# A_log loaded as four rows and transposed by TensorE, with the weight transfers issued at other places

## The chip, the cores and the metric

The kernel runs on one NeuronCore of a Trainium2 chip. Times are device microseconds (us) of one execution. The runs of one version lie 1 to 3% apart from the fastest to the slowest, so each version was run four to six times, next to runs of the kernel before on the same chip in the same rounds. A run that is over 1.5% above the fastest run of its own version counts as slow and is left out of ratios. Every ratio below is the mean time of one kernel's fast runs over the mean of the other's fast runs of the same rounds, with a 95% interval, so it is not quite the ratio of the medians that stand beside it. "Slower" means more than 2%; where the interval spans 2%, the record calls the run unclear.

Engines are PE (TensorE matmul), PEld (its weight load), DVE (VectorE), ACT (ScalarE), POOL (GpSimd) and SP (SyncE, which here only issues DMAs).

## The reference, cut to what matters

An RWKV-like attention feeds a gated state-space layer:

```python
# attention; r, k, v, w: (4, 8, 768, 48) float32, u: (8, 48)
for t in range(S):
    cur = einsum('bhd,bhe->bhde', u[None] * kt, vt)
    y[:, :, t] = einsum('bhd,bhde->bhe', rt, state + cur)
    state = wt[:, :, :, None] * state + einsum('bhd,bhe->bhde', kt, vt)
# x = y as (4, 768, 384); w_in: (384, 1024), A_log: (512,), w_out: (512, 384)
proj = x @ w_in
val, gate = proj[..., :512], proj[..., 512:]
a = exp(A_log)
for t in range(S):
    h = a * h + val[:, t, :]
    ys[:, t, :] = h
return (silu(gate) * ys) @ w_out
```

A_log is 512 words, 2 KB, of the 23.80 MB that the SP queue moves. It is used for the first time by the first scan over h.

## The kernel before

The kernel is hand-scheduled. The 24 chunks of 128 steps (12 units of two) and the layer behind them are cut into small pieces of work, each with a letter, and one long string says in which order they are issued. Each piece goes to the queue of its engine, and each engine takes its queue in order. The letters that matter here: `w r k v` load a unit's w and a chunk's r, k, v (SP queue); `l` takes the logarithm of w (ACT); `c j` are cumulative sums of it (PE); `K` scales k by an exponential (POOL; `H` on DVE); `m u d V` make the bonus term (`m u V` on POOL, `d` on DVE); `A Y S T t` are attention matmuls and transposes (PE); `+` adds the bonus on DVE and `*` adds it through PE; `g n` are the projections with w_in (PE), `h` the scan, `o` the output projection; `W` issues a third of w_in (256 KB, on POOL's queue, cast to bf16 on the way), `X` half of w_out; `0` loads u and A_log, `a` takes exp of A_log; `#` is a filler matmul whose result nobody uses; it only keeps PE from standing idle. A number behind a letter, as in w3 or k5, counts its occurrences from 0: w3 is unit 3's w, k5 chunk 5's k.

```python
loads = ctx.enter_context(tc.tile_pool(name="loads", bufs=6))
...
w_in_sb = const.tile([128, NT, 2 * DI], BF16)
w_out_sb = const.tile([128, NG, DM], BF16)
a_log = const.tile([128, NG], F32)              # NG = 4: 16 bytes in each partition
a_sb = const.tile([128, NG], F32)
u_sb = const.tile([C, H, D], F32)
...
def load(n, un, ci):                            # k, r, v: runs of 48 words (192 B)
    if (n, un) not in raw:
        raw[n, un] = loads.tile([C, 2, H, D], F32, tag=n, name=n)
    t = dict(k=k, r=r, v=v)[n]
    nc.sync.dma_start(out=raw[n, un][:, ci], in_=bass.AP(..., ap=[[D, C], [S * D, H], [1, D]]))

def load_w(un):                                 # w: runs of 96 words (384 B)
    raw["w", un] = loads.tile([C, H, 2, D], F32, tag="w", name="w")
    nc.sync.dma_start(out=raw["w", un], in_=bass.AP(..., ap=[[2 * D, C], [S * D, H], [1, 2 * D]]))

def load_w_in(T):
    nc.gpsimd.dma_start(out=w_in_sb[:, T], in_=moe_w_in[T * 128 : (T + 1) * 128, :])

def load_small():
    nc.sync.dma_start(out=u_sb, in_=bass.AP(..., ap=[[0, C], [1, H * D]]))
    nc.sync.dma_start(out=a_log, in_=moe_A_log.rearrange("(g p) -> p g", p=128),
                      allow_slow_non_contiguous=True)
...
def f_a():
    nc.scalar.activation(a_sb, a_log, Exp)
```

## Time and profile before

| | before |
|---|---|
| median of 3 runs (range) | 139.37 us (138.71 to 139.43) |
| span of the profiled run | 137.9 us |
| PE busy | 128.1 us, 93% |
| TensorE clock granted | full throughout |
| packets of the SP queue | 91488, for 23.80 MB |

The prediction shows the lines that locate the bound: PE nearly without idle time after about 35 us, and before that a start set by loads. The time that the packets took as a share of 16 engines' span: every packet's time counts in full, so in a short window a share can pass 1.

```profile
q1 hardware_dynamic: 91488, 23.80, 76.6%
```

### The profile page before, as it was taken

The numbers are of one execution on the slowest core, as the hardware profiler recorded it, in microseconds if no ns is written. First come the engines' busy times: TensorE is split into PE (matmuls) and PEld (weight loads), VectorE is DVE, ScalarE is ACT, GpSimd is POOL, SyncE is SP. The second block draws the span as 40 slices with busy tenths as digits, with TensorE's granted clock in tenths as the row PEclk, the third lists the DMA queues.
The fourth block names the chain that finished last, engine by engine and source line by source line (L and its number), as shares of the span: only waits on it lengthen the run. The fifth ranks groups of instructions, "written<-read, shape, count | busy, mean of one in ns | idle before, by whom it ended". The sixth has DMA issues, their size and how long they took to land.

```text
span 137.9 us, 3768 instructions
## 1 busy us (share of the span) xinstructions
PE 128.1 (93%) x1433; PEld 78.7 (57%) x1441; DVE 114.4 (83%) x206; ACT 105.6 (77%) x208; POOL 111.2 (81%) x116
## 2 busy tenths in 40 slices
PE   5999997698899999999999999999999899999990
PEld 2345453465555554766456756766666476676850
DVE  1261698589898799989989999999999899999950
ACT  3350935874987799999998999999999998554451
POOL 7652559998696599999999999999899998405960
PEclk9999999999999999999999999999999999999999
DMA  4998979999898998999999899898958631011344
GB/s 88 287 203 161 217 140 234 192 227 251 172 243 164 193 246 166 243 216 213 193 211 223 168 209 302 164 207 222 305 165 179 152 125 57 0 57 62 114 165 177
DMA packets 92481, 25.21 MB, mean 183 GB/s; under 512 B 88368, under 2 KB 92080, under 8 KB 92464
## 3 DMA queue, kind: packets, MB, share of 16 engines
q1 hardware_dynamic: 91488, 23.80, 76.6%
q0 software_dynamic: 976, 1.18, 5.2%
q8 instruction: 11, 0.18, 0.5%
q14 instruction: 6, 0.05, 0.1%
HBM read 21.43 MB, written 4.72 MB: 190 GB/s over the span
## 4 chain that ended last, share of the span: by engine, by line
PE 59%; SPq 12%; DMA 9%; DVE 5%; POOL 5%; issue 3%; ACT 3%; ACTq 0%; DVEq 0%; POOLq 0%
PE bank L403 18%; PE bank L445 10%; SPq L190 10%; PE bank L310 5%; PE bank L233 4%; DMA w_in_sb<-in_moe_w_in_dram 4%; PE bank L323 4%; PE bank L99 3%; DMA r<-in_r_dram 3%; PE bank L345 3%; DVE bank L427 2%; PE bank L367 2%; DMA k<-in_k_dram 2%; PE bank L342 2%; PE bank L350 2%
## 5 line engine op out<-in xcount | busy, mean ns | idle before, releaser
L403 PE MATMUL bank<-xT,w_in_sb 128*128 128x384 bf16 (+2 forms) x216 | 38.4, 309 | 1.9 <-DMA w_in_sb<-in_moe_w_in_dram 1.0
L331 DVE TENSOR_TENSOR At<-bank,mask 128x512 bf16<-128x512 f32 x48 | 30.4, 682 | 0.5 <-PE bank L323 0.4
L99 PE MATMUL bank<-fill 128*128 128x512 bf16 x85 | 25.3, 410 | 1.9 <-DVE fill L91 1.5
L403 PEld LDWEIGHTS <-w_in_sb 128*128 128x128 bf16 x216 | 18.3, 98 | 11.3 <-DMA w_in_sb<-in_moe_w_in_dram 1.4
L283 POOL TENSOR_TENSOR rk<-rk,u_sb 128x768 f32<-128x768 f32 (+1 forms) x13 | 21.9, 1687 | 2.8 <-DMA u_sb<-in_u_dram 2.6
L278 POOL TENSOR_TENSOR rk<-r,k 128x768 f32<-128x768 f32 (+1 forms) x13 | 21.9, 1688 | 2.5 <-DMA k<-in_k_dram 2.5
L293 POOL TENSOR_TENSOR VD<-v,dv 128x768 f32<-128x768 f32 (+1 forms) x13 | 17.9, 1378 | 5.0 <-DVE dv L288 4.9
L272 POOL TENSOR_TENSOR Qb<-r,EQ 128x384 bf16<-128x384 f32 x19 | 19.0, 1002 | 2.7 <-ACT EQ L266 2.1
L172 ACT COPY qk<-bank 128x1024 bf16<-128x1024 bf16 x19 | 19.7, 1036 | 0.5 <-PE bank L310 0.3
L445 PE MATMUL bank<-w_out_sb,s 128*128 128x384 bf16 x96 | 18.9, 326 | 0.1
L414 ACT ACTIVATE s<-bank 128x384 bf16<-128x384 f32 (+2 forms) x36 | 15.7, 463 | 3.7 <-PE bank L403 3.5
L272 POOL TENSOR_TENSOR Kb<-k,EK 128x384 bf16<-128x384 f32 x17 | 16.9, 997 | 1.5 <-ACT EK L266 1.1
L172 ACT COPY o<-bank 128x384 f32<-128x384 f32 x23 | 11.4, 494 | 4.1 <-PE bank L445 2.8
L99 PEld LDWEIGHTS <-fill 128*128 128x128 bf16 x93 | 8.5, 103 | 10.3 <-issue 3.1
L225 ACT ACTIVATE lwb<-w 128x768 bf16<-128x768 f32 x12 | 10.3, 862 | 4.7 <-DMA w<-in_w_dram 4.6
L440 DVE TENSOR_TENSOR s<-s,bank 128x384 bf16<-128x384 bf16 x24 | 12.8, 547 | 1.2 <-ACT c L436 0.9
L440 POOL TENSOR_TENSOR s<-s,h 128x384 bf16<-128x384 bf16 (+2 forms) x12 | 7.6, 675 | 6.3 <-DVE h L427 6.3
L427 DVE TENSOR_TENSOR_SCAN bank<-a_sb,bank 128x384 f32<-128x384 f32 x12 | 11.3, 956 | 1.4 <-PE bank L403 0.7
L427 DVE TENSOR_TENSOR_SCAN bank<-a_sb,c,bank 128x384 f32<-128x384 f32 x12 | 12.0, 1013 | 0.6 <-PE bank L403 0.6
L392 DVE TENSOR_TENSOR SE<-bank,E 128x384 bf16<-128x384 f32 x20 | 11.0, 548 | 0.9 <-PE bank L384 0.9
L288 DVE TENSOR_REDUCE dv<-rk 128x16 f32<-128x768 f32 (+1 forms) x13 | 11.5, 883 | 0.2 <-POOL rk L283 0.2
L361 DVE TENSOR_TENSOR yb<-bank,VD 128x384 bf16<-128x384 f32 x20 | 11.0, 550 | 0.8 <-PE bank L350 0.8
(74 smaller groups left out, 240.5 us busy)
## 6 DMA issues: line engine op xcount, KB each, us to landing
r<-in_r_dram SPq DMA_DIRECT2D x24, 192.0 KB, 4.3
w<-in_w_dram SPq DMA_DIRECT2D x12, 384.0 KB, 4.6
k<-in_k_dram SPq DMA_DIRECT2D x24, 192.0 KB, 4.3
v<-in_v_dram SPq DMA_DIRECT2D x24, 192.0 KB, 4.1
out_dram<-o SPq DMA_DIRECT2D x24, 192.0 KB, 1.9
w_in_sb<-in_moe_w_in_dram POOLq DMA_DIRECT2D x3, 256.0 KB, 5.4
w_out_sb<-in_moe_w_out_dram POOLq DMA_DIRECT2D x2, 192.0 KB, 4.5
u_sb<-in_u_dram SPq DMA_DIRECT2D x1, 192.0 KB, 4.6
```

The lines of the kernel that those rows point to most:

```text
L99: nc.tensor.matmul(t, fill[:, :128], fill, start=True, stop=True, skip_group_check=True)
L172: (nc.scalar.copy if e == "ACT" else eng[e].tensor_copy)(dst, src)
L272: eng[e].tensor_tensor(dst[un % 3][:, ci, :, :D], raw[src, un][:, ci], tl[ex, i], op=MUL)
L278: eng[e].tensor_tensor(tl["rk", un][:, c0:c1], raw["r", un][:, c0:c1], raw["k", un][:, c0:c1], op=MUL)
L283: eng[e].tensor_tensor(t, t, u_sb[:, None].broadcast_to([C, c1 - c0, H, D]), op=MUL)
L293: nc.gpsimd.tensor_tensor(tl["VD", un][:, c0:c1], raw["v", un][:, c0:c1], tl["dv", un][:, c0:c1, :, None].broadcast_to([C, c1 - c0, H, D]) ...
L331: nc.vector.tensor_tensor(At[:, hh], tl["A", i][hh], mask[:, None, :].broadcast_to([C, NP, C]), op=MUL)
L403: nc.tensor.matmul(ps, w_in_sb[:, T, col : col + 128], xT[b][:, T, x[0] : x[1]], start=(T == 0), stop=(T == NT - 1))
L414: nc.scalar.activation(sg[b, g][:, x[0] : x[1]], tl["g", b, x, g], Silu)
L427: nc.vector.tensor_tensor_scan(dst, a_sb[:, g : g + 1].broadcast_to([128, n]), ps, 0.0 if x[0] == 0 else tl["c", b, g], op0=MUL, op1=ADD)
L440: (nc.gpsimd if b == B - 1 else nc.vector).tensor_tensor(s, s, tl["h", b, x, g], op=MUL)
L445: nc.tensor.matmul(ps[:, :DM], sg[b, g][:, tt * 128 : (tt + 1) * 128], w_out_sb[:, g, :], start=(g == 0), stop=(g == NG - 1))
```

## The change

The intent: 512 single words are a costly way to bring 2 KB, and they stand in the queue early, when loads set the pace. Four rows of 512 bytes, transposed by PE against an identity matrix, take their place. The weights go out earlier, so that the first gate projection no longer waits for them, and the whole order is arranged anew around that.

```diff
-    a_log = const.tile([128, NG], F32)
+    a_rows = const.tile([NG, 128], F32)
     a_sb = const.tile([128, NG], F32)
     u_sb = const.tile([C, H, D], F32)
...
-        nc.sync.dma_start(out=a_log, in_=moe_A_log.rearrange("(g p) -> p g", p=128),
-                          allow_slow_non_contiguous=True)
+
+    def load_a():
+        nc.sync.dma_start(out=a_rows, in_=moe_A_log.rearrange("(g p) -> g p", p=128))
+
+    def f_at():
+        tl["at"] = bank(512)[:, :NG]
+        nc.tensor.transpose(tl["at"], a_rows, ident32[:NG, :NG])
+
+    def f_a():
+        nc.scalar.activation(a_sb, tl["at"], Exp)
...
-    put("a", f_a)
+    for letter, fn in zip("LRa", (load_a, f_at, f_a)):
+        put(letter, fn)
... the order, first three of eleven lines
-    "rwwkrlv############cjrl2k##c1Q2Hk1Pm#####tv0Hmw##########tj2r31qkHuP2r3##########t1dAqvx"
-    "Vbk###AualP##YwxmSprus#######Avdcjx1k2K1HW2+Vld########TQ3#cPWt1etbHmq##SvqYstW+V1ApTAxy"
-    "ubkx#####SrYA+vjsT3xwy#Y2g2KdSkigPgrstV+iv#npbghwiniShKYClksm###AzrnzTCv*hjyuTvYx23lke2Q"
+    "wrvkwl############cjr2r1Q32Hkbmkl10############cPt1w1pKrHm#########tvjquAk32Wdr2PVxL####"
+    "###tvWAWbkP#Ylpmwx##S*#RAsrcuxj1vYau32TdkPvlVd1K#########cH2+###tePSqktKsp1##AV1txbTAqm#"
+    "Yx###Se*AKsrjxTuY32vy2w*d#######gkgiPSr#tVgpvinisgbwhniSKlhAkYmnsrzzCCv####TxjQyYv2+ulhk"
...
```

More of the change, by code (lines that the diff above doesn't have):

```diff
@@ L33 @@
 ORDER = (
-    "rwwkrlv############cjrl2k##c1Q2Hk1Pm#####tv0Hmw##########tj2r31qkHuP2r3##########t1dAqvx"
-    "Vbk###AualP##YwxmSprus#######Avdcjx1k2K1HW2+Vld########TQ3#cPWt1etbHmq##SvqYstW+V1ApTAxy"
-    "ubkx#####SrYA+vjsT3xwy#Y2g2KdSkigPgrstV+iv#npbghwiniShKYClksm###AzrnzTCv*hjyuTvYx23lke2Q"
-    "####jzC*rdn2QcrbhtVT1kYe31zgC2HwKip#gSQ+Avsgmxcirni1nhrtuSvhlkz1#####jQsqwzKdb###Ac3xk2Q"
-    "t1TY2rVp1ty+SvqAsmgrxlSAYvisKxk###TnK*kYbhtQwyTn+yuzqTthvgqAemrgzigdiXgixniVjlvhnKXcSzYh"
-    "Q1k2Cs2u3rz*#####YCH1Tckb+tQe1TdvSyA1xgvqnmgwisghnKrohCiSVbkozfztkiYsKCqA+vgxQnfriSlujhw"
-    "TozAemows2x32cfn>1KSdfrY1jbhQktl+VnrzqostvhfKY32T2+QoqzTeSQleAstrfQxgqAknmxigvtghrKgiAiv"
-    "zouqx>Yitkf+Auqdc>jk1xnoV>hn>1Y>2hKo2>3CTfzQjvyzACf+K>Y2xbt>Qov32+TSfmdnq>cstkyhS1Vn1rTz"
-    "CoqhuYyYsfgCzb>o+KvigdAQg+SxVfAio>ixtmfTY>ysnb+nhqQYohKTTfgzyu>Syzti+gqsAgdiAigxVSigxYin"
-    "o+sTnhyTfYy>nzghnigzgi+nhonhfzTo>yhzingohzifngh>gzginihfgnzii>nhnnzohznohfzh>ohzfhzo>Fzz"
-    "of>o>f>f>"
+    "wrvkwl############cjr2r1Q32Hkbmkl10############cPt1w1pKrHm#########tvjquAk32Wdr2PVxL####"
+    "###tvWAWbkP#Ylpmwx##S*#RAsrcuxj1vYau32TdkPvlVd1K#########cH2+###tePSqktKsp1##AV1txbTAqm#"
+    "Yx###Se*AKsrjxTuY32vy2w*d#######gkgiPSr#tVgpvinisgbwhniSKlhAkYmnsrzzCCv####TxjQyYv2+ulhk"
+    "###T2jyrzC3Q*d##n2rcbhtVk3T1Ye1pCwg2KzgiHmSvsAg+rix#ciQnk1ShunrthlvKz1####jwqzQd32###Ask"
+    "K2tbxcrTVY11tpryS+qmAsgvlxTSvAiYQskxK###nk*YyQhtwbTnu+ytzqgrhTgiXveqgzXAdmrgiinxivjlVSkh"
+    "nckhK#YC1z2Q2s1H#####Yu*z3Cbc+T1TevtyQdS1AvqgKsgxrinQgwhnVSbohkoimzfrYsitCzfAwC+qugxTniv"
+    "lShjKvoemzAkos32xfcr2Y1QnrdfSlKjh>1twbVYsn2+2zk#oKqhtkQ3fo+qzTrTQSefAestvlQxAgqvKnxigrmt"
+    "g>hY>iguqz>A+okixitf>uAqcdvj1xn>Vorhn1>TK2Yhk2o3QfzjCC>yzAQ2+vYfxt3KbTo2+QqSdcnmfstynh1v"
+    "o1qVzTkShYyY>CfusgC>bzo>+ig+AKdgSKfxoi>AiVTfsYyx>tQnqT+nmhyTYohtufzgy>zbS+gisgqdAgixTVAi"
+    "SigyxYin+osnfhTY>ynzghgininz+ghoiofhzT>gfnhyz>iohnzggnihiznfghn>igznhoizhnnfznoh>zhofhzh"
+    "oz>FzozF>of>>f>"
 )
@@ L455, in f_st @@
         nc.sync.dma_start(out=out[b, tt * 128 : (tt + 1) * 128, :], in_=tl["o", b, tt])
-    def f_a():
-        nc.scalar.activation(a_sb, a_log, Exp)
     def ranges(b):
```

## The prediction

> **What bounds the kernel now.** I read the busy shares first, then two stretches of the span side by side, the chain of waits, and the DMA stream in fine windows. In the list of windows the columns are engine by engine busy us (instructions), then the TensorE clock, the DMA share and GB/s.
>
> ```profile
> PE 128.1 (93%) x1433; PEld 78.7 (57%) x1441; DVE 114.4 (83%) x206; ACT 105.6 (77%) x208; POOL 111.2 (81%) x116
> ...
> PEclk9999999999999999999999999999999999999999
> ```
> ```profile
> 0.00:35.00 35.00, 30.39 (x297) 15.70 (x301) 21.52 (x53) 18.66 (x36) 24.66 (x42) 1.00 0.97 201
> 35.00:134.50 99.50, 97.67 (x1136) 63.05 (x1140) 92.86 (x154) 86.49 (x172) 86.52 (x74) 1.00 0.79 177
> ```
> After 35 us PE idles 99.50 - 97.67 = 1.83 us in almost 100. Before 35 us it idles 4.61 us, 1.53 of them before its first instruction, so 3.08 in the middle. PE takes its queue in order and part of that queue is filler matmuls ("#", 93 of them, 25.3 us busy), which do nothing but run while inputs are awaited. So the end is when the real work starts in earnest, plus a full PE queue. The start is set by loads:
>
> ```profile
> 23.42 0.99 POOL Kb L272
> 24.41 0.68 POOL w_in_sb L211
> 25.11 0.84 POOL VD L293
> 25.96 0.92 POOL Qb L272
> 26.88 0.56 POOL w_in_sb L211
> 27.47 1.76 POOL rk L278
> 29.24 5.79 DMA w_in_sb<-in_moe_w_in_dram
> 35.07 0.34 PE bank L403
> ```
> This is the chain of waits (start, us, what). POOL is working without a gap, two weight issues of some 0.6 us are inside its queue, and the third weight slab, issued at 29.24, lands at 35.03. The first gate projection (letter g) waits for it: PE 1.0 us, its weight loads 1.4.
>
> Now the A_log load, from the SP queue in order of time and from the DMA in windows:
>
> ```profile
> 10.05 0.88 SPq L219 DMA_DIRECT2D u_sb<-in_u_dram  x1
> 10.97 0.43 SPq L221 DMA_DIRECT2D a_log<-in_moe_A_log_dram  x1
> 11.45 0.51 SPq L202 DMA_DIRECT2D w<-in_w_dram  x1
> 11.99 0.58 SPq L190 DMA_DIRECT2D r<-in_r_dram  x1
> 12.62 3.03 SPq L190 DMA_DIRECT2D k<-in_k_dram  x1
> ```
> ```profile
> 12.00:12.60 0.60, 0.60 (x10) 0.48 (x8) 0.00 (x0) 0.00 (x0) 0.16 (x1) 1.00 1.31 224
> 12.60:14.40 1.80, 1.80 (x22) 0.86 (x20) 0.00 (x0) 0.83 (x3) 0.00 (x0) 1.00 0.40 52
> 14.40:18.40 4.00, 3.92 (x47) 2.15 (x46) 3.42 (x7) 4.00 (x9) 2.79 (x3) 1.00 1.03 229
> ```
> Two kilobytes break the stream: for 1.8 us it moves 52 GB/s between stretches of 224 and 229, in 450 packets of 0.09 MB, and SP is stuck 3.03 us in the next load of k, where such an issue usually takes about 0.9. Those k rows land only at 19.76, where POOL has waited 1.55 us for them.
>
> **What the Trainium skill says.** "DMA: Bandwidth & Descriptors", section "Rules for kernel authors": a strided last dimension becomes one descriptor per element; its "Specifications" put the size for line rate at 512 B or more. The trace agrees: the dip above. The same page, "Issuing engines are not separate DMA queues": DMAs from several engines share the same 16 DMA engines and interleave. The trace agrees in that the DMA share is 0.97 over the first 35 us, so weights brought forward push something else back. "TensorE: Matmul & The Clock Gate", section "Part 4: PE-mode transpose": a transpose lands in PSUM and took about 275 to 390 ns for a bf16 128x128; here 8 bf16 transposes take 0.45 us in the chain, far less each. No row shows the float32 one of 4x128.
>
> **The change part by part.**
>
> A_log. Gone are 512 descriptors. At 201 GB/s the dip costs 1.8 x (1 - 52/201) = 1.3 us of stream (part of it may be the tail of u's load, so 1.0 to 1.4). Added are 4 rows, one transpose (I take 0.25 us, a guess below one 0.71 us pair of float32 matmuls) and an Exp from PSUM in place of one from SBUF (0.25 us, the a_sb row). SP's issue cost stays near 0.4.
>
> Weights. The three w_in issues move in POOL's queue from among V1, Q4 and m3 (24.4 to 29.2 us) to just after u0 and V0. u0 ended at 15.8; u now goes to the queue one load earlier, so the issues fall at about 14.5 to 17.5, and at 5.4 us each the slabs are there by 23. The wait at 35.07 is gone. But 768 KB now go ahead of k4, w3, r5, v3 and k5 (by counting the loads in order; from k6 on both orders have sent the same bytes). At 201 GB/s that is 3.9 us later, less 1.3 for A_log: about +2.6 us. In the landed bytes of the old run, w3 (number 4994 KB) comes at about 27.0, v3 at 28.8 and k5 at 29.8; less 1.3 these are 25.7, 27.5 and 28.5.
>
> Order and engines. I counted the letters. Fillers 93 to 97. The bonus goes by PE ("*") 6 times in place of 4; the new ones are chunks 0, 2 and 3, chunk 4 goes back to VectorE. A "*" costs PE 0.71 us (chain: L342 x2) and a filler 0.216 us (L99 x4, 0.86). PE's queue grows by 0.86 + 1.42 + 0.25 = 2.5 us. Split at the first gate: before it +1 filler, +3 "*", +1 transpose = 2.6 us; after it +3 fillers (0.65) and -1 "*" (0.71) = -0.06 us. The last copies get one more on VectorE; tail about unchanged.
>
> **Walk to the first gate.** Floor from PE alone: 35.07 - 3.08 + 2.6 = 34.6 us, with no wait left at all. With data: PE has chunk 1's output and T0 done by about 22 (24.2 before), then 9 fillers to 24.0, then sums c3, which need w3 (25.7) and its log (0.84): 26.5, a wait of 2.5 us. From there t3, S1, t4, A3, t5, T1, A4 and three fillers' places bring Y2 to about 30.9. By POOL's queue: K5 needs k5 (28.5), then V2 (1.48), and Y2 now takes V2 through PE: also 30.9. From Y2 to the gate PE still has 1.05 + 0.65 (3 fillers) + 0.33 + 0.33 + 0.75 + 0.19 + 0.37 + 1.5 (7 fillers) = 5.2 us, so 36.1. That is 1.0 us later than now. The landing times are good to 1.5 us at best, so 34.6 to 37.
>
> After the gate PE's content is the same. The stream is 1.3 us ahead there, POOL has had its weight issues behind it, and by my sum reaches u5 some 2 to 3 us sooner unless PE holds it. So perhaps half of the 1.83 us idle goes: -0.9. Sum: +1.0 - 0.06 - 0.9 = about 0, i.e. 139.4.
>
> I move this to 138.8: the schedule is plainly the output of a search in which such an order would have been kept for being quicker, and my walk assumes the weights go wholly ahead of the SP loads although the two queues interleave, which delays w3 and k5 too much.
>
> **Rivals.**
> 1. The stream gain flows through: early inputs come 1.3 us sooner, w3 and k5 are hardly late, the gate starts at 34.6 and later idle goes as well. For: SP's queue heads the chain of waits for the first 18 us. Against: 2.6 us more in PE's queue before the gate. It makes -0.5 - 1.8 = -2.3 us, 137.0. This is my bound for what the change can bring.
> 2. A new wait takes the old one's place: c3 on w3, or K5/V2 on k5, with the fillers executed in order before and after. For: DMA share 0.97. It makes +1 to +2 us without later recovery, 140.4 to 141.4.
> 3. The row load lands late (interleaved with the weights) and the transpose holds PE at about 20 us. For: it sits in PE's queue before A2 and c2. Against: 9 fillers and the wait for w3 come after it. It makes nothing unless over 2 us.
> 4. VectorE or ScalarE is the bound after 35 us, so nothing early matters. VectorE is busy 92.86 of 99.5: less than PE, but at 122.7 to 127.3 it carries the chain. It makes 139.
>
> **Range and chances.** Predicted 138.8 us, 8 in 10 between 137.1 and 140.6. Faster by over 2% means below 136.6, past the bound of rival 1: 0.06. Slower by over 2% means above 142.2: 0.04. Within 2%: 0.90.
>
> **What would show it.** A_log: no stretch near 52 GB/s around 13 us, no issue of 3 us at k3, k3's rows before 19. Weights: no DMA wait at the first gate; in its place waits for DMA at lwb (w3), Kb (k5) or VD around 24 to 30 us. PE: about 130.6 us busy, the gate's third matmul near 35 to 36, idle after it near 1 us. I am wrong if the gate starts before 34.5, if w3 and k5 come as early as before, or if PE's idle after the gate grows, which would mean that another engine sets the pace there.

## More of the kernel before

```profile
r<-in_r_dram SPq DMA_DIRECT2D x24, 192.0 KB, 4.3
w<-in_w_dram SPq DMA_DIRECT2D x12, 384.0 KB, 4.6
```

A share and a count give the time of one packet: 0.766 x 16 x 137.9 us / 91488 = 18.5 ns. Nearly all packets are runs of 192 or 384 bytes of r, k, v and w.

## The result, and the profile after

| | before | after |
|---|---|---|
| median of 4 runs (range) | 139.04 us (138.41 to 139.43) | 143.74 us (143.17 to 144.81) |
| ratio of fast runs | | 1.0351 [1.0273, 1.043]: slower |
| span of the profiled run | 137.9 us | 141.6 us |
| packet time in the SP queue | 18.5 ns | 21.7 ns |

From the page of the kernel after: the busy shares, TensorE's granted clock in 40 slices (tenths), and the SP queue.

```profile
PE 131.4 (93%) x1440; PEld 81.0 (57%) x1450; DVE 114.1 (81%) x205; ACT 104.9 (74%) x208; POOL 111.8 (79%) x117
...
PEclk9999998699999999999999999999999999999999
...
q1 hardware_dynamic: 90968, 23.80, 87.1%
```

```profile
w<-in_w_dram SPq DMA_DIRECT2D x12, 384.0 KB, 5.4
r<-in_r_dram SPq DMA_DIRECT2D x24, 192.0 KB, 4.9
```

Here are two surprises. The queue carries the same megabytes in 520 fewer packets, yet its packets fill 87.1% of the engines' span in place of 76.6%: each takes 0.871 x 16 x 141.6 / 90968 = 21.7 ns, 17% more. And the clock has a dent near 25 us.

Next, the windows of the kernel after: start and end, length, busy us (instructions) of PE, PEld, DVE, ACT and POOL, then the clock, the DMA share and GB/s.

```profile
12.00:16.00 4.00, 3.69 (x40) 1.83 (x39) 0.75 (x2) 1.60 (x4) 2.83 (x3) 1.00 0.98 217
...
20.00:23.00 3.00, 0.00 (x0) 0.00 (x0) 1.08 (x3) 0.58 (x2) 3.00 (x3) 1.00 1.13 183
23.50:27.00 3.50, 3.50 (x39) 1.95 (x34) 2.91 (x5) 1.22 (x4) 2.34 (x3) 0.51 1.00 219
...
39.76:138.20 98.44, 97.61 (x1139) 63.47 (x1142) 92.20 (x153) 85.69 (x171) 85.98 (x74) 1.00 0.88 173
```

The hole of 52 GB/s at 13 us is gone. PE stands idle for all of 20 to 23 us, and then runs at half the clock for 3.5 us. From the first gate on, it idles 98.44 - 97.61 = 0.83 us; from its gate on the kernel before idled 1.77. So the loss is all ahead of the gate. The timeline of that stretch in the kernel after (start, us, engine, line, what; in brackets the idle time just before it and who ended it):

```profile
23.03 0.22 PE L227 MATMUL bank<-ident,a_rows 4*128 4x4 f32 x1 [3.10 <-DMA a_rows<-in_moe_A_log_dram]
...
28.16 0.84 ACT L233 ACTIVATE lwb<-w 128x768 bf16<-128x768 f32 x1 [2.36 <-DMA w<-in_w_dram]
29.06 0.50 PE L241 MATMUL bank<-lwb,TE 64*128 64x384 bf16 x4 [0.53 <-ACT lwb L233]
31.44 1.00 POOL L280 TENSOR_TENSOR Kb<-k,EK 128x384 bf16<-128x384 f32 x1 [4.21 <-DMA k<-in_k_dram]
32.39 1.48 POOL L301 TENSOR_TENSOR VD<-v,dv 128x768 f32<-128x768 f32 x1
...
33.92 0.91 PE L350 MATMUL bank<-VD,ident 128*128 128x384 f32 x2
...
39.76 1.14 PE L411 MATMUL bank<-xT,w_in_sb 128*128 128x384 bf16 x6
```

The gate no longer waits for its weights. But w3 is there only at 28.16 and k5 at 31.44; V2 follows K5 in POOL's queue, Y2 takes V2's result through PE at 33.92, and another 5.8 us of PE's queue lie between that and the first gate at 39.76. Before, the third matmul of the first gate started at 35.07; here, at 0.16 us a matmul in the chain of waits, it starts near 40.1. PE's last matmul ends at 138.15 in place of 134.42, 3.7 us later.

Three things stand in that picture as suspects: the transpose that holds PE until 23.03 and costs it its clock, the 768 KB of weights ahead of w3 and k5, and the slow packets, which nothing in the prediction accounts for. The cast of w3 in the kernel before, to compare with:

```profile
24.03 0.84 ACT L225 ACTIVATE lwb<-w 128x768 bf16<-128x768 f32 x1 [1.14 <-DMA w<-in_w_dram]
```

### The profile page after: what moved, and what is told of

It reads as the page before. It is cut to its first block, busy times and chain, and to the rows that moved or that the text cites. A ratio compares the mean times of both kernels' runs of the same rounds, so it can differ in the third digit from the quotient of the medians.

```text
span 141.6 us, 3780 instructions
## 1 busy us (share of the span) xinstructions
PE 131.4 (93%) x1440; PEld 81.0 (57%) x1450; DVE 114.1 (81%) x205; ACT 104.9 (74%) x208; POOL 111.8 (79%) x117
## 3 DMA queue, kind: packets, MB, share of 16 engines
q1 hardware_dynamic: 90968, 23.80, 87.1%
## 4 chain that ended last, share of the span: by engine, by line
PE 64%; SPq 18%; DMA 5%; ACT 4%; DVE 2%; POOL 2%; issue 1%; POOLq 0%; DVEq 0%; ACTq 0%
PE bank L411 21%; SPq L190 13%; PE bank L453 9%; PE bank L99 6%; PE bank L318 5%; PE bank L331 4%; PE bank L241 4%; SPq L202 4%; DMA k<-in_k_dram 3%; PE bank L375 3%; PE bank L350 3%; PE bank L353 2%; PE bank L392 2%; PE bank L358 2%; DMA r<-in_r_dram 2%; ACT qk L172 2%
## 5 line engine op out<-in xcount | busy, mean ns | idle before, releaser
L99 PE MATMUL bank<-fill 128*128 128x512 bf16 x87 | 26.7, 421 | 2.0 <-DVE fill L91 1.5
L280 POOL TENSOR_TENSOR Kb<-k,EK 128x384 bf16<-128x384 f32 x19 | 18.9, 997 | 7.5 <-DMA k<-in_k_dram 6.5
L411 PEld LDWEIGHTS <-w_in_sb 128*128 128x128 bf16 x216 | 18.3, 98 | 9.4 <-issue 0.8
L286 POOL TENSOR_TENSOR rk<-r,k 128x768 f32<-128x768 f32 (+1 forms) x13 | 21.9, 1686 | 1.1 <-DMA k<-in_k_dram 1.0
L172 ACT COPY qk<-bank 128x1024 bf16<-128x1024 bf16 x18 | 18.6, 1032 | 3.9 <-PE bank L318 3.9
L280 POOL TENSOR_TENSOR Qb<-r,EQ 128x384 bf16<-128x384 f32 x18 | 17.8, 995 | 3.8 <-ACT EQ L274 3.8
L453 PE MATMUL bank<-w_out_sb,s 128*128 128x384 bf16 x96 | 18.5, 326 | 0.1
L99 PEld LDWEIGHTS <-fill 128*128 128x128 bf16 x97 | 9.2, 105 | 11.3 <-issue 4.2
L308 ACT CAST vb<-v 128x768 bf16<-128x768 f32 (+1 forms) x13 | 10.3, 796 | 2.6 <-DMA v<-in_v_dram 2.6
```

What stands on the lines that cost most here:

```text
L99: nc.tensor.matmul(t, fill[:, :128], fill, start=True, stop=True, skip_group_check=True)
L172: (nc.scalar.copy if e == "ACT" else eng[e].tensor_copy)(dst, src)
L280: eng[e].tensor_tensor(dst[un % 3][:, ci, :, :D], raw[src, un][:, ci], tl[ex, i], op=MUL)
L286: eng[e].tensor_tensor(tl["rk", un][:, c0:c1], raw["r", un][:, c0:c1], raw["k", un][:, c0:c1], op=MUL)
L411: nc.tensor.matmul(ps, w_in_sb[:, T, col : col + 128], xT[b][:, T, x[0] : x[1]], start=(T == 0), stop=(T == NT - 1))
L453: nc.tensor.matmul(ps[:, :DM], sg[b, g][:, tt * 128 : (tt + 1) * 128], w_out_sb[:, g, :], start=(g == 0), stop=(g == NG - 1))
```

## The experiments

### First four: the parts of the change apart

Theories at this point, by the letters of the expectations: (Q) the early weights push w3 and k5 back; (R) the row load lands late, and the transpose stalls PE and its clock. Each run does or undoes one part.

**Old order, A_log as rows.** The code of the kernel after with the order of the kernel before, weights at their old places:

```diff
-    ...tv0Hmw##... / ...###AualP##...
+    ...tv0LHmw##... / ...###ARualP##...      (L, R, a: rows load, transpose, exp)
```

> The old order of everything, with the four rows of A_log loaded where the single words were, transposed by PE after the second A (chunk 1), when they should long have landed. Theory Q (the weights sent early push back w3 and k5, and that is the loss): 138.3 to 139.5 us, the first gate at 34 to 35 us; the dip to 52 GB/s at 13 us goes, and what it gives is at most 1 us. Theory R (PE's wait for the rows and the halved clock after it are the loss): the same 138.3 to 139.5, with no PE wait for a_rows here. A time over 141 would say that the rows cost by themselves, which neither expects.

Measured: 141.93 us (141.2 to 143.17), before 139.75; ratio 1.0184 [1.0093, 1.0275]. Neither theory expected this. With the old order, the weights in their old places and 512 descriptors fewer, the kernel is still slower. Two of its four runs, 142.66 and 143.17, were granted a mean clock of 0.98 (in the one profiled, PE had waited 2.56 us for the third weight slab at 36.99, and the clock was halved from 38.3 to 41.8 us). The other two, at full clock, are 1.2% above the kernel before.

**New order, transpose late.** R moves behind Y3 and `a` behind the third `*`, so that PE reaches the first gates before it needs A_log's rows:

```diff
-    ...S*#RAsrcuxj1vYau32...  / ...TuY32vy2w*d#######gkg...
+    ...S*#Asrcuxj1vYu32...    / ...TuYR32vy2w*ad#######gkg...
```

> The changed kernel with the transpose and its Exp put off to just before the first gate, so that PE no longer waits 3.1 us for the rows and the clock should stay full. Theory Q: PE then waits for w3 and for V2 instead; k5 still lands at 30.5 to 31.5, the gate starts at 39 to 40, time 142.7 to 143.8. Theory R: the gate comes 3 to 5 us sooner, time 139 to 140.5.

Measured: 145.43 us (144.13 to 146.51); ratio 1.0395 [1.0297, 1.0492], against 1.0351 with the transpose in its place; slower than either theory expected. The run profiled serves for the place of the waits only. These are the clock line of its page and a line of its PE timeline:

```profile
PEclk9999999955999999999999999999999999999999
...
29.65 0.82 PE L241 MATMUL bank<-lwb,TE 64*128 64x384 bf16 x4 [5.19 <-ACT lwb L233]
```

PE no longer waits for A_log; it waits 5.19 us for w3 instead. The 3.1 us stall at the transpose was time that PE would have spent waiting a little later anyhow. Theory R falls as far as the place of the transpose goes. The clock is not tested by this run, though the expectation meant it to be: PE's longer wait halved it again, from 28.6 to 35.5 us, and the fast runs were granted 0.973 to 0.986, no more than those of the kernel after (0.976 to 0.988). The ledger takes it up.

**New order, weights back among later work.** W0 after u2, W1 after K3, W2 after K5:

```diff
-    ...uAk32Wdr2PVxL...  / ...tvWAWbkP...  / ...xj1vYau32...    / ...Vd1K####...   / ...qktKsp1...
+    ...uAk32dr2PVxL...   / ...tvAbkP...    / ...xj1vYauW32...   / ...Vd1KW####...  / ...qktKWsp1...
```

> The changed kernel with the three w_in issues put back into GpSimd's later queue (after u2, K3 and K5), the transpose left where PE waits for the rows. Theory Q: k5 lands by 28, V2 is done by 31, the gate starts at 36 to 37, time 139.5 to 141. Theory R: PE still waits for the rows (perhaps 1 us less, since the weights are not in the way), time 142 to 143.7.

Measured: 142.17 us (141.92 to 142.58); ratio 1.0195 [1.0129, 1.0261]. The early weights cost 1.0351 / 1.0195 = 1.015, but two per cent stay, more than I expected; all four runs had the full clock.

**Old order, weights early.** The kernel before (A_log as words) with W0 after u0 and W1, W2 after V0:

```diff
-    ...qkHuP2r3...   / ...AqvxVbk...     (and three W further on)
+    ...qkHuWP2r3...  / ...AqvxVWWbk...
```

> The kernel before, single-word A_log and all, with only the three w_in issues moved up to after u0 and V0 as in the changed kernel. Theory Q: slower, 141 to 143.5 us, since k5 and w3 land 3 us later and the old order needs them as well; no clock loss is needed for it. Theory R: 138 to 139.5, as the wait of 1 us for the third slab goes and nothing else changes.

Measured: 142.36 us (141.9 to 142.93); ratio 1.0207 [1.0137, 1.0278]. The clock line of its page, and its timeline (ACT and POOL) with the waits:

```profile
PEclk9999999659999999999999999999999999999999
...
27.21 0.84 ACT L225 ACTIVATE lwb<-w 128x768 bf16<-128x768 f32 x1 [4.28 <-DMA w<-in_w_dram]
30.12 1.80 POOL L278 TENSOR_TENSOR rk<-r,k 128x768 f32<-128x768 f32 x1 [3.76 <-DMA k<-in_k_dram]
```

In the kernel before, the same cast of w3 started at 24.03. So theory Q holds in both orders, and costs some 2%. Here this takes in a loss of clock, which the expectation had thought unnecessary: PE stood 3.77 us before 27.16, the clock was halved from 25.5 to 32.3 us, and all four runs were granted 0.976 to 0.988. The early weights set that off, but this run doesn't part the two. Theory Q leaves two per cent of the change unexplained, and these sit in whatever the change has in common with the first run: rows in place of words, with nothing else moved.

### A new theory: the tiles have moved

What the first and third runs share with the kernel after, and the fourth doesn't, is slow packets. The page gives a share of 83.7% for the first and 86.0% for the third, against 74.3% for the fourth. These are the windows from 8 to 12 us, in which the stream runs without a stop, of the first run and of a run described below, the same kernel with a pad of 32 bytes:

```profile
8.00:12.00 4.00, 4.00 (x28) 1.95 (x27) 1.36 (x4) 1.34 (x4) 1.96 (x2) 1.00 1.44 186
```

```profile
8.00:12.00 4.00, 4.00 (x28) 2.00 (x28) 1.80 (x5) 1.32 (x4) 2.95 (x3) 1.00 1.17 226
```

The engines are busier (1.44 against 1.17) and move less (186 against 226 GB/s). This pair shows it at its largest; over the first 35 us, three pairs of the same kernel with its tiles shifted and not move 199 against 209, 187 against 201 and 190 against 207 GB/s, with shares of 1.13 against 1.01, 1.07 against 0.97 and 1.14 against 1.00. The same loads are under way in both, A_log's rows among them, so no operation that the change adds explains it. What is left is the *declaration*. I looked up the addresses that the build gives to the tiles. `a_log`, 16 bytes in each partition, took 32; `a_rows`, which uses four partitions only, takes 512 bytes of every partition's address range. So each tile allocated later moves up by 480 bytes:

| bytes from the start of a partition | before | after |
|---|---|---|
| a_log / a_rows | 45504 | 45504 |
| u_sb | 45568 | 46048 |
| first tiles of the load pool | r 47104, w 65536, k 83968, v 102400 | w 47584, r 66016, v 84448, k 102880 |
| these modulo 512 | 0 | 480 |
| these modulo 64 | 0 | 32 |

Theory S: loads made of runs of 192 and 384 bytes land more slowly in tiles that start 32 bytes past a multiple of 64. The test is a tile that nobody uses, declared after `a_sb`:

```diff
     a_sb = const.tile([128, NG], F32)
+    pad = const.tile([128, 8], F32)       # 32 bytes; [128, 16], 64 bytes, in the second run
     u_sb = const.tile([C, H, D], F32)
```

**The kernel before with a pad of 32 bytes** (load tiles 32 past a multiple of 512; nothing else changes):

> The kernel before with one unused tile of 32 bytes per partition put in ahead of u_sb and the load tiles; every instruction is the same, only the SBUF addresses behind it move by 32, so that the tiles of r, k, v and w start at 32 past a multiple of 64, as they do in the changed kernel. Theory S (the 480 bytes that the rows tile adds move all load tiles off a multiple of 64, each DMA packet takes longer, and this is a good part of the loss): 141 to 142.5 us, and the hardware queue's share goes from 77 to 83 or more per cent with the same 91488 packets. Theories Q and R (issue places, wait for the rows): 138.4 to 140, as before.

Measured: 142.54 us (141.83 to 144.43), before 139.12; ratio 1.0222 [1.016, 1.0283]. An unused tile of 32 bytes costs about 2%, at full clock. (The run profiled, the slowest of the four, counts as slow, at a clock of 0.998.) Page lines of this run and of the next:

```profile
q1 hardware_dynamic: 91488, 23.80, 84.6%
```

**The kernel before with a pad of 64 bytes** (the rival theory: any shift, or any other neighbourhood of tiles, does it):

> The same with an unused tile of 64 bytes, so that the load tiles start at a multiple of 64 again, though no longer of 512. Theory S, if it is 64 that counts: 138.4 to 140, queue share 75 to 78 per cent. If it is a multiple of 128 or 512 that counts: as slow as with 32. Theories Q and R: 138.4 to 140.

```profile
q1 hardware_dynamic: 91488, 23.80, 78.8%
```

Measured: 140.32 us (139.06 to 141.11); ratio 1.0071 [0.9998, 1.0144]: same. Time and share lie just above what was expected. Not the shift but where it leads makes the difference, and a multiple of 64 is enough, or nearly. The packet times of all fourteen profiles fall apart in the same way: 18.3 to 18.6 ns in the eight with load tiles at multiples of 512, 19.1 in this one, 20.8 to 21.7 in the five at 32 bytes past a multiple of 64.

**The kernel after with a pad of 32 bytes** (load tiles back at multiples of 512):

> The changed kernel, order and all, with the unused tile of 32 bytes, which puts the load tiles at a multiple of 512 again (480 + 32). Theory S with Q: 140.5 to 142.3, queue share back to 76 to 79 per cent, w3 and k5 landing 1.5 to 3 us sooner than in the changed kernel, while some loss of the early weights stays. Theory Q alone or R alone: 143 to 144.5.

Measured: 141.19 us (140.59 to 141.77); ratio 1.0142 [1.0076, 1.0208]. The queue's share falls to 74.8%, its packets to 0.748 x 16 x 139.3 / 90968 = 18.3 ns. An unused tile wins back more than half of the loss: 1.0351 / 1.0142 = 1.021. Its timeline:

```profile
21.20 0.22 PE L228 MATMUL bank<-ident,a_rows 4*128 4x4 f32 x1 [1.83 <-DMA a_rows<-in_moe_A_log_dram]
...
26.39 0.84 ACT L234 ACTIVATE lwb<-w 128x768 bf16<-128x768 f32 x1 [2.95 <-DMA w<-in_w_dram]
27.28 0.50 PE L242 MATMUL bank<-lwb,TE 64*128 64x384 bf16 x4 [2.07 <-ACT lwb L234]
29.11 0.99 POOL L281 TENSOR_TENSOR Kb<-k,EK 128x384 bf16<-128x384 f32 x1 [3.72 <-DMA k<-in_k_dram]
...
37.47 1.14 PE L412 MATMUL bank<-xT,w_in_sb 128*128 128x384 bf16 x6
```

Everything of the chain stands where it stood, 1.8 to 2.3 us sooner. PE's wait for the rows is 1.8 us now, and the clock stays at full speed throughout the run profiled. The Trainium skill, "TensorE: Matmul & The Clock Gate", section "What's actually happening", has the clock halved after an idle window of about 3.4 us. The runs here differ from it in size: after 3.1 us without work PE ran at 0.51 of its clock for 3.5 us, and in the run with the weights early in the old order the clock fell at 25.5 us, when PE had stood for 2.1 us. After the stops of 1.83 and 2.07 us in this timeline it stayed full.

**Old order, rows, pad of 32 bytes** (the first run of all, mended):

> The old order with the rows load and the transpose (the first experiment, 141.9 us), with the unused 32 bytes. Theory S: back to 138.0 to 139.7, that is as before or up to 1 us faster, as the rows spare the stream the dip at 13 us. If the rows or the transpose cost by themselves: 141 to 142.5 again.

Measured: 139.47 us (137.48 to 140.78), ratio 0.9933 [0.9837, 1.0029] of the two of its four runs that count as fast; with all four, whose mean is 139.30, against a mean of 139.20 for the kernel before, it is 1.001. So the rows by themselves are no slower than the words, and against 1.0184 without the pad the shift costs 1.8 to 2.5% in this order too, with the halved clock of two runs without the pad in it.

### Third call: what is left, and a better version

**New order, pad, weights back** (the third run with the pad):

> The changed kernel with the unused 32 bytes (load tiles at a multiple of 512) and the three w_in issues back among u2, K3 and K5; the transpose stays where it was. If the shift of the tiles and the early weights are together the loss: k5 lands by 26, the first gate starts at 33.5 to 35.5 us, time 138.0 to 139.8. If the new order of the rest, or the wait for the rows, also costs: 140.3 to 141.5, as with the pad alone (141.2).

Measured: 139.21 us (138.78 to 140.6), before 139.43; ratio 0.9985 [0.9927, 1.0043]. With the shift and the early weights undone, the new order is as fast as the old, to within 0.7%. Its w3:

```profile
23.22 0.84 ACT L234 ACTIVATE lwb<-w 128x768 bf16<-128x768 f32 x1 [1.55 <-DMA w<-in_w_dram]
```

**The same with the transpose late** (R and `a` as in the second run):

> The same with the transpose put off to just before the first gate. With the weights back the rows should land early enough (PE waited only 0.5 us for them without the pad), so the same as the run before within 0.7 us. If it is faster by more than 1 us, the place of the transpose does matter once the inputs come sooner.

Measured: 139.65 us (138.99 to 140.92); ratio 1.001 [0.9952, 1.0069]. The place of the transpose makes nothing here; but in the run before the rows had landed in time (transpose at 19.43, no wait), so there was no stall to take away.

**Old order, rows, pad, W2 directly after W1** (an attempt at a version that beats both):

```diff
-    ...t1etbHmq##SvqYstW+V1ApTA...   / ...Q3#cPWt1...
+    ...t1etbHmq##SvqYst+V1ApTA...    / ...Q3#cPWWt1...
```

> A try for a version better than both: the old order with the rows, the transpose after A1, the 32 bytes of padding, and only the third w_in issue moved up beside the second. The third slab should land 1.7 us sooner, before the gate asks for it at 32 to 33 us; m3 starts 0.6 us later. 137.0 to 139.0 us. If 256 KB sooner pushes a needed load back, 139.5 to 141.

Measured in five rounds: 139.01 us (137.28 to 141.08); ratio 0.9892 [0.9827, 0.9956]. Two of its six runs count as slow; with all six the means are 138.91 and 139.59, a ratio of 0.995. At its first gate PE no longer waits for the weights, and the gate's first matmul starts at 33.47. It is half a per cent to one ahead of the kernel before, by the 2% rule the same, and not told apart from the version with rows and pad alone (0.9933).

**New order with the words load** (the code of the kernel before, the order of the kernel after less L and R; A_log goes out at `0`, so the tiles are aligned):

```diff
-    ...PVxL####...  / ...S*#RAsrc...
+    ...PVx####...   / ...S*#Asrc...
```

> The changed kernel's order with the old load of 512 single words (placed with u_sb, as before) and without the transpose, so that the load tiles are at a multiple of 512 by themselves; the early weights stay. It is the rows part undone. If the shift is the whole cost of the rows part: 140.5 to 142.2, near the padded changed kernel (141.2), the dip at 13 us adding up to 1 us and PE's wait for the rows gone. If the rows cost anything more than the shift (the wait, the transpose): 138.5 to 140.

Measured: 143.75 us (143.38 to 146.3); ratio 1.0279 [1.0224, 1.0333], 1.5 us above the top of what I expected. Against the same order with rows and aligned tiles (1.0142), the words cost 1.4% here. All its runs were granted 0.976 to 0.985 of the clock, the padded kernel 0.997 or more: in the run profiled PE waits 4.55 us for w3 and then has half its clock from 28.8 to 35.6 us. So the 1.4% holds a loss of clock too. Its run profiled is a slow one, but the place where it sticks is plain; the SP queue, and a window of that time:

```profile
12.04 4.13 SPq L190 DMA_DIRECT2D v<-in_v_dram  x1
```

```profile
12.00:14.00 2.00, 2.00 (x18) 1.03 (x16) 0.59 (x2) 0.26 (x1) 1.35 (x2) 1.00 0.28 57
```

SP is stuck 4.13 us in the third load behind the 512 words, and the DMA engines are used to 0.28 meanwhile. The row load takes the empty engines away, as the change intended: in the same two microseconds the padded kernel has 0.93 and 249 GB/s. SP's long issue it only shortens: the same load takes 2.62 us there, with no words in the queue.

### The ledger

| step | how | ratio |
|---|---|---|
| load tiles 32 bytes off a multiple of 64 | after / after with pad | 1.021 |
| | third run / the same with pad | 1.021 |
| | before with pad of 32 / before | 1.022 |
| | first run / the same with pad | 1.018 to 1.025 |
| weights early | after with pad / the same, weights back | 1.016 |
| | after / after with weights back | 1.015 |
| | before with weights early / before | 1.021 |
| all else (rows, order, fillers, bonus through PE) | new order, pad, weights back / before | 0.9985 |

Ratios of ratios come partly from different chips. Each is good to about 1%; that the shift comes out alike four times is what makes it firm. The three steps in the new order multiply to 1.035 by construction. A check that isn't: the pieces measured in the *old* order give 1.0222 x 1.0207 x 0.9933 = 1.036 (1.044 with all four runs of the last), and the change itself gave 1.0351.

The clock: the second and third rows compare kernels that had 0.995 or more of it on both sides, so the shift costs 2% without any loss of clock. So does the first row of the early weights, with 1.6%. These alone, 1.0195 for the third run times 1.0142 / 0.9985 for the weights, give 1.036, and the kernel after, with its dent, 1.0351: the dent adds nothing that shows within that 1%. The timeline says why: after it PE still waits 0.53 us for w3, at 29.06.

What the two causes do is told by four profiled runs (us; the cast of w3 on ACT, the third sums on PE, the first gate matmul, the end of PE's last matmul). The run with weights back was profiled in its slowest execution, 140.6 us, so its end is late by about 1.4. Single profiles scatter: the two runs with the old order, rows and pad send the same loads up to w3, and cast it at 22.70 and 24.02.

| | w3 cast | c3 | gate | end |
|---|---|---|---|---|
| before | 24.03 | 24.93 | 33.60 | 134.42 |
| new order, pad, weights back | 23.22 | 24.12 | 35.75 | 135.31 |
| after with pad | 26.39 | 27.28 | 37.47 | 135.85 |
| after | 28.16 | 29.06 | 39.76 | 138.15 |

In these profiles early weights push w3 back by 3.2 us and the gate by 1.7; the shift pushes w3 back by another 1.8 and the gate by 2.3. In the other pairs the shift makes 0.3 to 1.6 on w3 and 0.5 to 2.0 on the gate, always in this direction.

## Why the prediction was wrong

It gave 138.8 us, a range to 140.6, and 0.04 to slower; the median is 143.74. By its own steps:

- **A_log: "Gone are 512 descriptors", 1.3 us of stream.** This is the step that failed most. The hole at 13 us did go. But the step priced the operations alone and not the declaration: the new tile moves every later tile by 480 bytes. With rows, aligned tiles and late weights, four profiles cast w3 at 22.70 to 24.02, so 0 to 1.3 us sooner than the 24.03 before, where the step has 1.3; in the new order (23.22) it is 0.8. The shift, which the step doesn't have, adds 1.8 in the change itself. So the term came out as +1.0 in place of -1.3. The reading "the DMA share is 0.97" was right for before and was carried over to a kernel in which, over the same 35 us, it became 1.14 while the rate fell from 201 to 190 GB/s. The reading of SP's 3.03 us as the words' doing was too simple: with rows in the old order and the pad the same issue still takes 2.12 us, and in the kernel after one of 2.80 stands at its place in the queue.
- **Weights: 768 KB, 3.9 us later.** The mechanism was right and the size nearly: the prediction's w3 at 27.0 is 3.0 us later than 24.03, and between the two aligned kernels in the new order it moves by 3.2. (The prediction gives the sum of both terms as +2.6, and then walks on with 25.7, which is +1.7; aligned it is 26.39, +2.4.) The 28.16 of the trace, in place of 25.7, is 24.03 - 0.8 + 3.2 + 1.8, by construction of the table. The gate stopped waiting for weights, as said. k5 was put at 28.5; aligned it is used at 29.11, in the kernel after at 31.44.
- **The walk.** With aligned tiles it held in kind and roughly in size: c3 after a wait of 2.07 us (2.5 predicted), V2 ending at 31.54 and Y2 at 31.73 (30.9), the gate at 37.47 (36.1). In the kernel after, the gate is at 39.76. Of these 3.7 us, in the two profiles, 2.3 are the shift; 1.4 the walk had too low.
- **After the gate, -0.9.** Right: 0.83 us idle in place of 1.77.
- **"I move this to 138.8".** Wrong by itself. The argument that a search would only keep a faster order is no reading of the profile, and it pulled the sum of 139.4 away from what the profile said. Even with aligned tiles the kernel takes 141.19, just out of the range; rival 2, a new wait in the old one's place, had 140.4 to 141.4. So the early weights alone bring it to the edge of the range or just out (one of the four runs, at 140.59, lies inside), and the shift takes it past 2%.
- **Rival 3.** The prediction let it make "nothing unless over 2 us". The transpose held PE 3.1 us and cost it half its clock for 3.5 us, and still made nothing that shows: with the transpose moved out of the way the time is no better (1.0395 against 1.0351), since PE only waits later for w3 and loses its clock there. That the halved clock costs nothing in the kernel after is read from the ledger and from the wait of 0.53 us that is left behind it.
- **Its own signs.** "PE busy about 130.6": 131.4, with some of it at the halved clock, and 129.9 with the pad. "The third matmul near 35 to 36": it came near 40.1, the first sign that the walk's inputs were late. "k3's rows before 19": GpSimd got them at 19.77, as late as before (19.76), and with the pad at 18.71. None of the three "I am wrong if" came about: none of them asked whether w3 and k5 come later than the walk has them.

What stays open: how the shift slows a packet. The pad of 32 bytes moves all later tiles, not the load tiles alone; that the loads are what suffers is read from the packet times and the queue share. GpSimd's products and VectorE's masks keep their durations (1686 against 1688 ns, 684 against 682). No run settles between a rule of 64-byte lines and one of 256-byte pieces; the 19.1 ns at 64 bytes past a multiple of 512, one profile, lean to the pieces.

## What to carry to other kernels

A changed tile declaration moves every tile behind it, so before a diff's operations are priced, compare the addresses before and after, and keep the destinations of loads with short runs (here 192 and 384 bytes) at multiples of 64 bytes; a pad that nobody uses was worth 2% here. When the same bytes take a larger share of the DMA engines, divide share by packets first: a stream can be slower with no transfer added. A bulk transfer moved forward when the stream is full takes its time from whatever was going to land in that stretch, and a wait seen at one instruction is worth only what the next wait doesn't take back.

## What the Trainium skill lacked or had wrong

- **Where in SBUF a load lands.** "SBUF — State Buffer", section "Operand start alignment", deals with which starts are legal, and says of its runs that they timed nothing. Here loads of runs of 192 and 384 bytes into tiles 32 bytes off a multiple of 64 took 21.7 ns a packet in place of 18.3 (the kernel after and the same with the pad), and cost 2.1% of the kernel. A warning about time is missing there.
- **The likely reason, not applied to it.** "DMA: Bandwidth & Descriptors", section "How a descriptor splits into AXI transactions", says that a transaction "must start from a 256B-aligned address". The page speaks of where a transaction reads; here it is the written side that moved, and that it is cut in the same way is assumed. An estimate from that: for four neighbouring runs of 192 bytes, 6 pieces become 7, and for two of 384, 4 become 5, when the tile starts 32 bytes past a multiple of 64 in place of a multiple of 256. With 73728 and 12288 such runs in the kernel this is 135168 pieces against 159744, 18% more; the packets took 13 to 18% more in the four pairs. At 64 bytes past, only the runs of 384 gain, 4.5% by the same count, and the packets took 0.788 x 16 x 138.4 / 91488 = 19.1 ns, 3% more. The sizes agree, but no run separates it from other rules of alignment.
- **What a load of single words does to the loads behind it.** The same page, where the prediction quotes it on single words, counts the descriptors; it doesn't say that the engines then stand half empty while SP is held in a later load: 3.03 us in the kernel before and 4.13 us in the new order with words, for 2 KB, with the engines at 0.40 and 0.28. A long issue alone is no sign of it: with rows and aligned tiles the same issues take 2.12 and 2.62 us, with the engines at 0.88 and 0.93.
- **How short a stop halves the clock.** "TensorE: Matmul & The Clock Gate", section "What's actually happening", has about 3.4 us. Here the clock fell after stops of 2.56 and 3.10 us, and once 2.1 us into a stop of 3.77.
